# Out projection with the tokens as the moving side: 512-wide matmuls, rows restored by 16-bit DMA transposes

## Chip, cores and metric

One core of a Trainium2 chip. The metric is the device time of one launch in microseconds (us); less is better. The kernel before takes 814.0 us (median of 3 runs, 813.29 to 814.13). Engines: PE multiplies matrices, PEld is its weight load, DVE is VectorE, ACT is ScalarE, POOL is GpSimd, SP issues DMAs.

## The reference

Four batches, each with q, k, v of 6016 x 256. A 256 x 256 attention matrix per batch from column-normalised q and k, v times it, then a gated feed-forward block on all 24064 tokens:

```python
qn = q / (norm(q, axis=1) + 1e-6);  kn = k / (norm(k, axis=1) + 1e-6)
a  = softmax(kn^T @ qn / tau)              # 256 x 256 per batch
x  = v @ a                                 # 24064 x 256 over all batches
out = (silu(x @ w_gate) * (x @ w_val)) @ w_out    # hidden width 1536
```

## The kernel before

`a` is folded into the weights (`Wg`, `Wv`), so a chunk of 4x128 tokens (the last of a batch has 3x128) passes three products: gate, value, out. A chunk has 12 steps, one per 128 of the hidden width. In each step PE does two gate matmuls and two value matmuls for this chunk, then four out matmuls for the chunk before. ACT makes the silu, DVE the product `sv`. In the background q and k of the next batch are squared (DVE, ACT), summed (POOL) and multiplied.

```python
class OutStage:                                  # one per chunk; cut
    def emit(self, count):
        for _ in range(count):
            j, f = divmod(self.at, FH)           # j: 128 tokens, f: 128 of the hidden width
            if f == 0 and j % 2 == 0:
                self.o_ps = psum_o.tile([P, 2, C], FP32, tag="o")
            nc.tensor.matmul(self.o_ps[:, j % 2, :],
                             self.sv[:, f, j * P:(j + 1) * P],     # stationary: tokens
                             w_out_sb[:, f, :],                    # moving: 256 columns
                             start=(f == 0), stop=(f == FH - 1))
            # ... after two j: one fp32 copy (ACT for the first pair, DVE for the second), one store

for gi, (b, ci) in enumerate(allc):              # 48 chunks
    for f in range(FH):
        g_ps, v_ps, mv = gv_matmuls(b, ci, f)    # 4 matmuls, 512 wide
        silu = gv_silu(g_ps, mv)
        gv_product(f, sv, silu, v_ps, mv)
        if prev is not None: prev.emit(prev.cm)  # 4 out matmuls, 256 wide
        if b + 1 < B: background(b + 1, ci * FH + f)
        # ... load_v two chunks ahead
    prev = OutStage(b, ci, sv)
```

Of the kernel before, what the change touches and what calls it, by code (L numbers as in the profile page):

```python
# [8 lines left out]
FP32 = mybir.dt.float32  # L9
BF16 = mybir.dt.bfloat16  # L10
FP8 = mybir.dt.float8e5
ALU = mybir.AluOpType
ACT = mybir.ActivationFunctionType
DR = mybir.MatmulPerfMode.DoubleRow
# [3 lines left out]
def kernel(  # L18
# [11 lines left out]
    nc = tc.nc  # L30
    P = 128

    B, N, C = q.shape
    D, DFF = moe_w_gate.shape
    assert C == D and C == 2 * P
    CH = C // P
    FH = DFF // P
# [8 lines left out]
    CS = 4  # L46
# [3 lines left out]
    chunks = [(s, min(CS, NS - s)) for s in range(0, NS, CS)]  # L50
    NCH = len(chunks)
    STEPS = NCH * FH
    groups = [(s, min(4, NS - s)) for s in range(0, NS, 4)]
# [9 lines left out]
    svpool = ctx.enter_context(tc.tile_pool(name="svpool", bufs=2))  # L63
    silupool = ctx.enter_context(tc.tile_pool(name="silupool", bufs=4))
    opool = ctx.enter_context(tc.tile_pool(name="opool", bufs=4))
    dram = ctx.enter_context(tc.tile_pool(name="dram", bufs=4, space=bass.MemoryType.DRAM))

    psum_gv = ctx.enter_context(tc.tile_pool(name="psum_gv", bufs=2, space=bass.MemoryType.PSUM))
    psum_o = ctx.enter_context(tc.tile_pool(name="psum_o", bufs=2, space=bass.MemoryType.PSUM))
# [23 lines left out]
    w_out_sb = const.tile([P, FH, C], BF16)  # L93
# [5 lines left out]
    def load_qk(b, g, which, gl=groups):  # L99
        if b not in qk_tiles:  # L100
            q_sb = qkpool.tile([P, NS, C], FP8, tag="q_sb")
            k_sb = qkpool.tile([P, NS, C], FP8, tag="k_sb")
            qk_tiles[b] = (q_sb, k_sb)
# [3 lines left out]
            out=dst[:, gs:gs + gm, :],  # L107
            in_=src[b].rearrange("(p s) c -> p s c", s=NS)[:, gs:gs + gm, :])

    def load_v(b, ci):  # L110
        cs, cm = chunks[ci]
        mv = cm * P
        vb = dram.tile([CS * P, C], BF16, tag="vb")
        nc.gpsimd.dma_start(  # L114
            out=vb[:mv, :].rearrange("(p s) c -> p (s c)", s=cm),
            in_=v[b, cs * P:cs * P + mv, :].rearrange("(p s) c -> p (s c)", s=cm))
        vT = vpool.tile([P, CH, CS * P], BF16, tag="vT")
        nc.sync.dma_start_transpose(out=vT[:, :, :mv], in_=vb[:mv, :])
        vt_ready[(b, ci)] = vT
# [16 lines left out]
    def evacuate_first_v(h):  # L136
        nc.vector.tensor_copy(vt_ready[(0, 0)][:, h, :], state["vt_ps"][:, h, :])
# [82 lines left out]
    def first_softmax(b):  # L220
        kq, ink = state[b, "kq"], state[b, "ink"]
        inq = work.tile([P, CH], FP32, tag="inq")
        first_root(inq, state[b, "cols"])
        s_f = work.tile([P, CH, C], FP32, tag="s_f")
        nc.vector.tensor_mul(s_f[:, 0, :], kq[:, 0, :], ink)
        nc.vector.tensor_scalar_add(inq, in0=inq, scalar1=1e-6)
        nc.vector.reciprocal(inq, inq)
        if inv_tau != 1.0:
            nc.vector.tensor_scalar_mul(inq, in0=inq, scalar1=inv_tau)
        nc.vector.tensor_mul(s_f[:, 1, :], kq[:, 1, :], ink)  # L230
        rs = psum_m.tile([P, CH], FP32, tag="misc")
        keep_warm(1)
        row_eps(rs)
        transpose_first_v()
        keep_warm(2)
        for h in range(CH):
            evacuate_first_v(h)
        exT = attn.tile([P, CH, C], BF16, tag="exT")
        state[b, "exT"] = exT
        for jh in range(CH):  # L240
            nc.scalar.activation(exT[:, jh, :], s_f[:, jh, :], ACT.Exp,
                                 scale=inq[:, jh:jh + 1])


        def row_sum(jh):
            for ih in range(CH):
                nc.tensor.matmul(rs[:, ih:ih + 1], exT[:, jh, ih * P:(ih + 1) * P],
                                 ones_bf[:, 0:1], start=False,
                                 stop=(jh == CH - 1), skip_group_check=True)

        units = []
        for u in range(2 * CH):
            unit_ps = psum_gv.tile([P, HW], FP32, tag="gv"[u % 2])
            units.append(unit_ps)
        row_sum(0)
        wp_matmul(b, 0, 0, units[0], lo)
        wp_matmul(b, 1, 0, units[1], lo)
        wp_matmul(b, 2, 0, units[2], lo)
        row_sum(1)
        finish_rs(b, rs)  # L260
        for u, jh in ((0, 1), (1, 1), (2, 1), (3, 0), (3, 1)):
            wp_matmul(b, u, jh, units[u], lo)
        for u in range(4):
            wp_evacuate(b, u, units[u], lo, u % 2 == 1)
        for u in range(2):
            wp_unit(b, u, psum_o, "o", hi)
        nc.scalar.preload_act_table(ACT.Silu)

    def norm_acc(b, t):
# [5 lines left out]
        if t == 0:  # L275
            acc_new = work.tile([P, 2, C], FP32, tag="acc")
            state[b, "acc"] = acc_new
            nc.gpsimd.tensor_tensor(out=acc_new, in0=sq[:, 0, :, :], in1=sq[:, 1, :, :],  # L278
                                    op=ALU.add)
            return  # L280
        acc = state[b, "acc"]
        for s in range(pm):
            nc.gpsimd.tensor_tensor(out=acc, in0=acc, in1=sq[:, s, :, :], op=ALU.add)  # L283

    def split3(src, shape, tag):
# [6 lines left out]
        nc.gpsimd.tensor_copy(hi, src)  # L292
        nc.gpsimd.tensor_tensor(out=rest, in0=src, in1=hi, op=ALU.subtract)
        nc.gpsimd.tensor_copy(mid, rest)
        nc.gpsimd.tensor_tensor(out=lo, in0=rest, in1=mid, op=ALU.subtract)
        return hi, mid, lo
# [4 lines left out]
    def norm_cols(b):  # L301
# [8 lines left out]
        nc.vector.tensor_copy(inv, cs)  # L310
        nc.gpsimd.tensor_tensor(out=inv, in0=inv, in1=half, op=ALU.pow)  # L311
        nc.gpsimd.tensor_scalar_add(inv, in0=inv, scalar1=1e-6)
        nc.gpsimd.tensor_tensor(out=inv, in0=inv, in1=minus, op=ALU.pow)
        state[b, "inv"] = inv
# [97 lines left out]
    def gv_matmuls(b, ci, f):  # L412
        cs, cm = chunks[ci]
        mv = cm * P
        Wg, Wv = state[b, "W"]
        vT = vt_ready[(b, ci)]
        fs = slice(f * P, (f + 1) * P)
        g_ps = psum_gv.tile([P, CS * P], FP32, tag="g")
        v_ps = psum_gv.tile([P, CS * P], FP32, tag="v")
        for dst, W in ((g_ps, Wg), (v_ps, Wv)):  # L420
            for kk in range(CH):
                nc.tensor.matmul(dst[:, :mv], W[:, kk, fs], vT[:, kk, :mv],  # L422
                                 start=(kk == 0), stop=(kk == CH - 1))
        return g_ps, v_ps, mv
# [6 lines left out]
    def gv_product(f, sv, silu, v_ps, mv):  # L431
        nc.vector.tensor_mul(sv[:, f, :mv], silu[:, :mv], v_ps[:, :mv])  # L432

    class OutStage:


        def __init__(self, b, ci, sv):
            cs, self.cm = chunks[ci]
            self.sv = sv

            pat = "(p s) c -> p s c" if (b, ci) == (0, 0) else "(s p) c -> p s c"
            r0 = b * N + cs * P
            self.dst = out[r0:r0 + self.cm * P, :].rearrange(pat, p=P)
            self.at = 0
            self.n = self.cm * FH
            self.o_ps = None

        def emit(self, count):
            for _ in range(count):
# [41 lines left out]

    LOAD0, SQ0 = 9, 21
    plan = [[] for _ in range(STEPS)]
    for g in range(len(groups)):
        plan[LOAD0 + 5 * g].append((load_qk, g, 0))
        plan[LOAD0 + 5 * g].append((load_qk, g, 1))
    for t in range(NP):
        step = SQ0 + (5 * t) // 2
        plan[step].append((norm_acc, t))
# [14 lines left out]
        plan[S1 + 36 + (u * 3) // 2].append((wp_unit, u))  # L514

    def background(b, step):
        for what, *args in plan[step]:
            what(b, *args)

    def load_w(c0, c1):  # L520
        cols = slice(c0, c1)
# [5 lines left out]
    allc = [(b, ci) for b in range(B) for ci in range(NCH)]  # L527
    VT_AHEAD = 2
# [19 lines left out]
    load_w(0, HW)  # L548
    load_w(HW, WP)
    load_v(*allc[1])  # L550
    for wc in range(1, NWC):
        load_w(wc * WP, (wc + 1) * WP)
    nc.gpsimd.dma_start(out=w_out_sb, in_=moe_w_out.rearrange("(h l) d -> l h d", l=P))
# [2 lines left out]
    for g, which, gl in order:  # L556
# [23 lines left out]
        if which == 0:  # L580
# [6 lines left out]
            if G_COLS <= g < NQ - 2:  # L587
                keep_warm(NQ - 2 - g)
    first_softmax(0)
    prev = None  # L590
    for gi, (b, ci) in enumerate(allc):
        sv = svpool.tile([P, FH, CS * P], BF16, tag="sv")
        for f in range(FH):
            g_ps, v_ps, mv = gv_matmuls(b, ci, f)


            us = range(2 * f + 2, min(2 * f + 4, len(wp_units))) if gi == 0 else ()
            part = hi if f == 0 else full
            for u in us[:1]:
                wp_unit(0, u, psum_o, "o", part, on_dve=True)  # L600
            silu = gv_silu(g_ps, mv)
            for u in us[1:]:
                wp_unit(0, u, psum_o, "o", part, on_dve=(f == 0))
            gv_product(f, sv, silu, v_ps, mv)
            if prev is not None:
                prev.emit(prev.cm)
            if b + 1 < B:
                background(b + 1, ci * FH + f)
            if f == 0 and gi + VT_AHEAD < len(allc):
                load_v(*allc[gi + VT_AHEAD])  # L610
        prev = OutStage(b, ci, sv)
    prev.finish()


# [1 line left out]
_INS = ['q', 'k', 'v', 'tau', 'moe_w_gate', 'moe_w_val', 'moe_w_out']  # L616
# [31 lines left out]
```

## Time and profile before

| | kernel before |
|---|---|
| time, median (range) | 814.0 us (813.29 to 814.13) |
| PE busy, waits of PE after 48 us | 98%, none |
| DVE, ACT, POOL busy | 65%, 53%, 32% |
| 16 DMA engines busy | 47% of the span by packet times |

The lines that carry this are in the prediction.

### The profile page before, as it was taken

How to read it: one execution, taken by the hardware profiler on the slowest of the kernel's cores; microseconds unless marked ns; L12 is line 12 of the kernel's file. 1: busy time of each engine (PE TensorE's matmuls, PEld its weight loads, DVE VectorE, ACT ScalarE, POOL GpSimd, SP SyncE). 2: the span in 40 equal slices, each digit the busy share in tenths (PEclk: the TensorE clock that was granted, in tenths of full speed). 3: DMA queues.
4: the chain of work that ended last, by engine and by line, in shares of the span. 5: the costliest groups of instructions: out<-in, count | busy, mean ns of one | idle time of the engine just before them, and what ended most of it. 6: DMA issues, size and time to landing. Idle time of an engine off the chain costs nothing.

```text
span 811.5 us, 13757 instructions
## 1 busy us (share of the span) xinstructions
PE 796.4 (98%) x5047; PEld 489.0 (60%) x5047; DVE 524.1 (65%) x795; ACT 433.9 (53%) x757; POOL 262.7 (32%) x320
## 2 busy tenths in 40 slices
PE   4999999999999999999999999999999999999998
PEld 2656666665566666666565666666556566665666
DVE  4777777657556777756655677765765555555554
ACT  4665655545555656545545556654555544444543
POOL 4415887323000888723000488752300000000000
PEclk9999999999999999999999999999999999999999
DMA  9994875319211778325812378531952122122101
GB/s 89 144 154 76 107 105 88 78 34 154 74 40 46 97 101 106 74 65 97 126 40 59 53 87 120 90 79 32 182 96 66 46 51 54 53 40 65 50 27 59
DMA packets 92308, 64.99 MB, mean 80 GB/s; under 512 B 52737, under 2 KB 89857, under 8 KB 91489
## 3 DMA queue, kind: packets, MB, share of 16 engines
q0 software_dynamic: 18144, 27.41, 29.1%
q1 hardware_dynamic: 73952, 36.65, 17.8%
q8 instruction: 39, 0.64, 0.3%
q14 instruction: 29, 0.23, 0.1%
q10 hardware_dynamic: 144, 0.07, 0.0%
HBM read 79.04 MB, written 36.70 MB: 143 GB/s over the span
## 4 chain that ended last, share of the span: by engine, by line
PE 96%; DMA 3%; issue 0%; DVE 0%; POOL 0%; POOLq 0%
PE o_new L456 30%; PE g_ps L422 30%; PE v_ps L422 30%; PE ps L391 2%; DMA q_sb<-in_q_dram 2%; PE kq_new L151 2%; DMA k_sb<-in_k_dram 1%; PE ps L381 0%; PE last_ps L480 0%; PE ss_new L178 0%; PE kq_new L156 0%; PE unit_ps L391 0%; PE cs L307 0%; POOL k_sb L106 0%; PE cols L191 0%
## 5 line engine op out<-in xcount | busy, mean ns | idle before, releaser
L432 DVE TENSOR_TENSOR sv<-silu,v_ps 128x512 bf16<-128x512 bf16 (+1 forms) x576 | 388.3, 674 | 263.1 <-ACT silu L428 260.4
L428 ACT ACTIVATE silu<-g_ps 128x512 bf16<-128x512 f32 (+1 forms) x576 | 338.7, 588 | 323.4 <-PE g_ps L422 291.9
L456 PE MATMUL o_new<-w_out_sb,sv 128*128 128x256 bf16 x2244 | 337.2, 273 | 0.0
L422 PE MATMUL g_ps<-vT,Wg 128*128 128x512 bf16 (+1 forms) x1128 | 330.7, 375 | 0.0
L422 PE MATMUL v_ps<-vT,Wv 128*128 128x512 bf16 (+1 forms) x1128 | 330.4, 374 | 0.0
L456 PEld LDWEIGHTS <-sv 128*128 128x128 bf16 x2244 | 219.6, 98 | 140.6
L422 PEld LDWEIGHTS <-Wv 128*128 128x128 bf16 x1152 | 112.7, 98 | 130.7 <-ACT Wv L403 0.2
L283 POOL TENSOR_TENSOR acc_new<-acc_new,sq 128x512 f32<-128x512 f32 x135 | 158.3, 1173 | 42.7 <-DVE sq L273 34.3
L422 PEld LDWEIGHTS <-Wg 128*128 128x128 bf16 x1152 | 109.6, 98 | 25.0
L273 DVE TENSOR_TENSOR sq<-q_sb 128x512 bf16<-128x512 fp8e5 x72 | 67.0, 930 | 0.0
L278 POOL TENSOR_TENSOR acc_new<-sq 128x512 f32<-128x512 bf16 x3 | 3.5, 1155 | 152.0 <-DVE sq L273 152.0
L274 ACT ACTIVATE sq<-k_sb 128x512 bf16<-128x512 fp8e5 x72 | 44.2, 614 | 0.0
L465 ACT COPY o_sb<-o_new 128x512 f32<-128x512 f32 x48 | 28.1, 586 | 14.9 <-PE o_new L456 14.5
L151 PE MATMUL kq_new<-k_sb,q_sb 128*128 128x512 fp8e5 x184 | 31.6, 298 | 1.0 <-DMA q_sb<-in_q_dram 0.9
L467 DVE COPY o_sb<-o_new 128x512 f32<-128x512 f32 (+1 forms) x47 | 31.3, 666 | 0.0
L106 POOL DMA_DIRECT2D q_sb<-in_q_dram x45 | 25.3, 562 | 14.8 <-DMA k_sb<-in_k_dram 9.9
L106 POOL DMA_DIRECT2D k_sb<-in_k_dram x42 | 22.8, 544 | 10.4 <-DMA w_out_sb<-in_moe_w_out_dram 5.5
L114 POOL DMA_DIRECT2D vb<-in_v_dram x47 | 24.0, 514 | 5.3 <-DMA vb<-in_v_dram 3.5
L178 PE MATMUL ss_new<-sq,ones_bf 128*128 128x256 bf16 x83 | 14.6, 332 | 11.1 <-ACT sq L168 11.1
L151 PEld LDWEIGHTS <-q_sb 128*128 128x256 fp8e5 x184 | 21.8, 140 | 2.8 <-DMA q_sb<-in_q_dram 2.0
L178 PEld LDWEIGHTS <-ones_bf 128*128 128x128 bf16 x83 | 9.2, 116 | 15.0 <-issue 11.0
L311 POOL TENSOR_TENSOR inv<-inv,half 128x4 f32<-128x4 f32 x3 | 3.1, 1036 | 36.7 <-DVE inv L310 36.7
(94 smaller groups left out, 198.3 us busy)
## 6 DMA issues: line engine op xcount, KB each, us to landing
out_dram<-o_sb SPq DMA_DIRECT2D x92, 256.0 KB, 2.5
vb<-in_v_dram POOLq DMA_DIRECT2D x43, 256.0 KB, 5.5
q_sb<-in_q_dram POOLq DMA_DIRECT2D x36, 128.0 KB, 4.5
k_sb<-in_k_dram POOLq DMA_DIRECT2D x33, 128.0 KB, 5.7
k_sb<-in_k_dram POOLq DMA_DIRECT2D x5, 256.0 KB, 9.0
q_sb<-in_q_dram POOLq DMA_DIRECT2D x4, 256.0 KB, 18.4
w_out_sb<-in_moe_w_out_dram POOLq DMA_DIRECT2D x1, 768.0 KB, 13.6
vb<-in_v_dram POOLq DMA_DIRECT2D x4, 192.0 KB, 3.9
```

Source lines behind the costliest of these rows:

```text
L106: nc.gpsimd.dma_start(out=dst[:, gs:gs + gm, :], in_=src[b].rearrange("(p s) c -> p s c", s=NS)[:, gs:gs + gm, :])
L114: nc.gpsimd.dma_start(out=vb[:mv, :].rearrange("(p s) c -> p (s c)", s=cm), in_=v[b, cs * P:cs * P + mv, :].rearrange("(p s) c -> p (s c)" ...
L151: nc.tensor.matmul(kq[:, jh, :], q_sb[:, ps:ps + 2, js], k_sb[:, ps:ps + 2, :], start=(t == 0 and jh == 0), stop=last, perf_mode=DR, skip_ ...
L273: nc.vector.tensor_mul(sq[:, :pm, 0, :], q_sb[:, ps:ps + pm, :], q_sb[:, ps:ps + pm, :])
L274: nc.scalar.activation(sq[:, :pm, 1, :], k_sb[:, ps:ps + pm, :], ACT.Square)
L283: nc.gpsimd.tensor_tensor(out=acc, in0=acc, in1=sq[:, s, :, :], op=ALU.add)
L422: nc.tensor.matmul(dst[:, :mv], W[:, kk, fs], vT[:, kk, :mv], start=(kk == 0), stop=(kk == CH - 1))
L428: nc.scalar.activation(silu[:, :mv], g_ps[:, :mv], ACT.Silu)
L432: nc.vector.tensor_mul(sv[:, f, :mv], silu[:, :mv], v_ps[:, :mv])
L456: nc.tensor.matmul(self.o_ps[:, j % 2, :], self.sv[:, f, j * P:(j + 1) * P], w_out_sb[:, f, :], start=(f == 0), stop=(f == FH - 1))
L465: nc.scalar.copy(o_sb[:, :m, :], self.o_ps[:, :m, :])
L467: nc.vector.tensor_copy(o_sb[:, :m, :], self.o_ps[:, :m, :])
```

## The change

Its intent is to halve the number of out matmuls: `w_out` becomes the stationary side and the tokens move, 512 at a time. The result then stands in columns (256 channels by tokens), and must be turned to rows. The DMA transpose takes 16-bit data, so each fp32 half is copied as two 16-bit planes, stored to DRAM, transposed back and stored as fp32. The last two chunks keep the old stage. To make room for these transfers, q and k of later batches are loaded over a longer time, and v passes through two fixed DRAM buffers and is transposed six steps after its load.

```diff
+class OutColumns:                               # cut
+    def step(self):                             # two matmuls per step
+        h, f = divmod(self.at, FH)
+        nc.tensor.matmul(self.o_ps[h][:, :self.mv], w_out_sb[:, f, h * P:(h + 1) * P],
+                         self.sv[:, f, :self.mv], start=(f == 0), stop=(f == FH - 1))
+    def copy(self, h):                          # at steps 5 and 11 of the chunk
+        halves = self.o_ps[h].bitcast(U16).rearrange("p (n t) -> p t n", t=2)
+        nc.scalar.copy(pl[:, 0, :self.mv], halves[:, 0, :self.mv])
+        nc.vector.tensor_copy(pl[:, 1, :self.mv], halves[:, 1, :self.mv])
+    def spill(self, h):                         # 2 steps later, SP
+        nc.sync.dma_start(out=rows[...], in_=self.planes[h][...])
+    def transpose(self, h):                     # 3 steps later, SP
+        nc.sync.dma_start_transpose(out=self.ot[...], in_=self.planes[h][...])
+    def store(self):
+        nc.sync.dma_start(out=self.dst, in_=self.ot[:, :self.cm, :].bitcast(FP32))
 ...
-        vb = dram.tile([CS * P, C], BF16, tag="vb")
+        vb = vb_tiles[(b * NCH + ci) % 2]
 ...
+            if b + 1 < B:                       # q and k of batch b + 1, half of them earlier
+                for what, *args in early_loads[step]: what(b + 1, *args)
 ...
-        prev = OutStage(b, ci, sv)
+        prev = (OutColumns if gi < len(allc) - 2 else OutStage)(b, ci, sv)   # shortened
```

More of the change, by code (lines that the diff above doesn't have):

```diff
@@ L11 @@
 FP8 = mybir.dt.float8e5
+U16 = mybir.dt.uint16
 ALU = mybir.AluOpType
@@ L65 @@
     opool = ctx.enter_context(tc.tile_pool(name="opool", bufs=4))
+    ocpool = ctx.enter_context(tc.tile_pool(name="ocpool", bufs=2))
+    plpool = ctx.enter_context(tc.tile_pool(name="plpool", bufs=4))
     dram = ctx.enter_context(tc.tile_pool(name="dram", bufs=4, space=bass.MemoryType.DRAM))
+    dram_v = ctx.enter_context(tc.tile_pool(name="dram_v", bufs=1, space=bass.MemoryType.DRAM))
     psum_gv = ctx.enter_context(tc.tile_pool(name="psum_gv", bufs=2, space=bass.MemoryType.PSUM))
@@ L108, in load_qk @@
             in_=src[b].rearrange("(p s) c -> p s c", s=NS)[:, gs:gs + gm, :])
+    vb_loaded = {}
+    vb_tiles = []
+    for n in range(2):
+        vb_new = dram_v.tile([CS * P, C], BF16, tag="vb%d" % n)
+        vb_tiles.append(vb_new)
     def load_v(b, ci):
@@ L116, in load_v, with transpose_v @@
             in_=v[b, cs * P:cs * P + mv, :].rearrange("(p s) c -> p (s c)", s=cm))
+        vb_loaded[(b, ci)] = vb
+    def transpose_v(b, ci):
+        mv = chunks[ci][1] * P
+        vb = vb_loaded.pop((b, ci))
         vT = vpool.tile([P, CH, CS * P], BF16, tag="vT")
@@ L432, in gv_product, with out_rows, __init__ @@
         nc.vector.tensor_mul(sv[:, f, :mv], silu[:, :mv], v_ps[:, :mv])
+    def out_rows(b, ci):
+        cs, cm = chunks[ci]
+        pat = "(p s) c -> p s c" if (b, ci) == (0, 0) else "(s p) c -> p s c"
+        r0 = b * N + cs * P
+        return out[r0:r0 + cm * P, :].rearrange(pat, p=P)
+    class OutColumns:
+        def __init__(self, b, ci, sv):
+            self.cm = chunks[ci][1]
+            self.mv = self.cm * P
+            self.sv = sv
+            self.dst = out_rows(b, ci)
+            self.at = 0
+            self.o_ps = [None] * CH
+            self.planes = [None] * CH
+            self.ot = None
+        def step(self):
+            for _ in range(CH):
+                h, f = divmod(self.at, FH)
+                if f == 0:
+                    o_new = psum_o.tile([P, CS * P], FP32, tag="o")
+                    self.o_ps[h] = o_new
+                nc.tensor.matmul(self.o_ps[h][:, :self.mv],
+                                 w_out_sb[:, f, h * P:(h + 1) * P],
+                                 self.sv[:, f, :self.mv],
+                                 start=(f == 0), stop=(f == FH - 1))
+                self.at += 1
+        def copy(self, h):
+            halves = self.o_ps[h].bitcast(U16).rearrange("p (n t) -> p t n", t=2)
+            pl = plpool.tile([P, 2, CS * P], U16, tag="pl")
+            nc.scalar.copy(pl[:, 0, :self.mv], halves[:, 0, :self.mv])
+            nc.vector.tensor_copy(pl[:, 1, :self.mv], halves[:, 1, :self.mv])
+            self.planes[h] = pl
+        def spill(self, h):
+            rows = dram.tile([2 * P, CS * P], U16, tag="rows%d" % h)
+            nc.sync.dma_start(
+                out=rows[:, :self.mv].rearrange("(p t) n -> p t n", t=2),
+                in_=self.planes[h][:, :, :self.mv])
+            self.planes[h] = rows
+        def transpose(self, h):
+            if self.ot is None:
+                ot_new = ocpool.tile([P, CS, 2 * C], U16, tag="ot")
+                self.ot = ot_new
+            nc.sync.dma_start_transpose(
+                out=self.ot[:, :self.cm, h * 2 * P:(h + 1) * 2 * P],
+                in_=self.planes[h][:, :self.mv])
+        def store(self):
+            nc.sync.dma_start(out=self.dst, in_=self.ot[:, :self.cm, :].bitcast(FP32))
@@ L434 @@
     class OutStage:
         def __init__(self, b, ci, sv):
-            cs, self.cm = chunks[ci]
+            self.cm = chunks[ci][1]
             self.sv = sv
-            pat = "(p s) c -> p s c" if (b, ci) == (0, 0) else "(s p) c -> p s c"
-            r0 = b * N + cs * P
-            self.dst = out[r0:r0 + self.cm * P, :].rearrange(pat, p=P)
+            self.dst = out_rows(b, ci)
             self.at = 0
@@ L446, in __init__, with step @@
             self.o_ps = None
+        def step(self):
+            self.emit(self.cm)
         def emit(self, count):
@@ L493 @@
     plan = [[] for _ in range(STEPS)]
+    first_loads = [[] for _ in range(STEPS)]
+    early_loads = [[] for _ in range(STEPS)]
+    late_loads = [[] for _ in range(STEPS)]
+    half_g = len(groups) // 2
     for g in range(len(groups)):
-        plan[LOAD0 + 5 * g].append((load_qk, g, 0))
-        plan[LOAD0 + 5 * g].append((load_qk, g, 1))
+        for which in range(2):
+            first_loads[LOAD0 + 5 * g].append((load_qk, g, which))
+            step = 7 + 11 * (g - half_g)
+            if step < 0:
+                early_loads[step + STEPS].append((load_qk, g, which))
+            else:
+                late_loads[step].append((load_qk, g, which))
     for t in range(NP):
@@ L516, in background @@
     def background(b, step):
-        for what, *args in plan[step]:
+        loads = first_loads if b == 1 else late_loads
+        for what, *args in loads[step] + plan[step]:
             what(b, *args)
+        if b + 1 < B:
+            for what, *args in early_loads[step]:
+                what(b + 1, *args)
     def load_w(c0, c1):
@@ L550 @@
     load_v(*allc[1])
+    transpose_v(*allc[1])
     for wc in range(1, NWC):
@@ L589, with at_step @@
     first_softmax(0)
+    later = {}
+    def at_step(n, what, *args):
+        later.setdefault(n, []).append((what, args))
     prev = None
@@ L593 @@
         for f in range(FH):
+            now = gi * FH + f
             g_ps, v_ps, mv = gv_matmuls(b, ci, f)
@@ L605 @@
             if prev is not None:
-                prev.emit(prev.cm)
+                prev.step()
             if b + 1 < B:
@@ L610 @@
                 load_v(*allc[gi + VT_AHEAD])
-        prev = OutStage(b, ci, sv)
+                at_step(now + 6, transpose_v, *allc[gi + VT_AHEAD])
+            for what, args in later.pop(now, ()):
+                what(*args)
+        if gi < len(allc) - 2:
+            prev = OutColumns(b, ci, sv)
+            n0 = (gi + 1) * FH
+            for h in range(CH):
+                n = n0 + FH // CH * (h + 1) - 1
+                at_step(n, prev.copy, h)
+                at_step(n + 2, prev.spill, h)
+                at_step(n + 5, prev.transpose, h)
+            at_step(n0 + 22, prev.store)
+        else:
+            prev = OutStage(b, ci, sv)
     prev.finish()
```

## The prediction

> **What bounds the kernel now.** I read the busy shares and the chain that ended last first, then PE's waits, then the groups, then the timeline.
>
> ```profile
> PE 796.4 (98%) x5047; PEld 489.0 (60%) x5047; DVE 524.1 (65%) x795; ACT 433.9 (53%) x757; POOL 262.7 (32%) x320
> ...
> PE 96%; DMA 3%; issue 0%; DVE 0%; POOL 0%; POOLq 0%
> ```
>
> The chain is PE for 96% of the span; the DMA part is the loading before about 28 us. All waits of PE in the execution:
>
> ```profile
> PE ss_new L178 <- ACT sq L168: 11.1, 6, 7.3
> PE kq_new L151 <- DMA q_sb<-in_q_dram: 0.9, 2, 0.5
> ```
>
> Both lines are of the prologue (columns: us in total, times, longest). From 48 us on PE waits for nothing, so only PE's own stream can be shortened. The matmuls of the timeline, start and length first:
>
> ```profile
> 190.22 0.60 PE L456 MATMUL o_new<-w_out_sb,sv 128*128 128x256 bf16 x4
> 190.65 0.59 PE L422 MATMUL g_ps<-vT,Wg 128*128 128x512 bf16 x2
> 191.09 0.59 PE L422 MATMUL v_ps<-vT,Wv 128*128 128x512 bf16 x2
> 191.52 0.60 PE L456 MATMUL o_new<-w_out_sb,sv 128*128 128x256 bf16 x4
> ```
>
> One step (one of 12 slices of the hidden width) is 1.30 us in thirds of 0.43: gate, value, out. The lengths overlap, so I use distances between starts: over all starts in the trace 109.2 ns after a 256-wide out matmul (1652 pairs of neighbours), 216.0 ns after a 512-wide one, 162.5 ns after a 384-wide one. Cross-check: the chain gives o_new 30.2% of 811.5 us, over 2244 matmuls 109.2 ns.
>
> ```profile
> L456 PE MATMUL o_new<-w_out_sb,sv 128*128 128x256 bf16 x2244 | 337.2, 273 | 0.0
> L456 PEld LDWEIGHTS <-sv 128*128 128x128 bf16 x2244 | 219.6, 98 | 140.6
> L465 ACT COPY o_sb<-o_new 128x512 f32<-128x512 f32 x48 | 28.1, 586 | 14.9 <-PE o_new L456 14.5
> L467 DVE COPY o_sb<-o_new 128x512 f32<-128x512 f32 (+1 forms) x47 | 31.3, 666 | 0.0
> ```
>
> A weight load takes 98 ns, less than the 109 ns of the matmul that it runs beside; it is hidden. The 337.2 us in the first row are not PE time to be won.
>
> **What the Trainium skill says.** "TensorE: Matmul & The Clock Gate", section "Wait — 56ns, not 53.3ns?": warm matmuls follow each other at N ÷ 2.4 GHz plus about 2.5 ns, fixed per matmul. That is 109.2 ns for 256 and 215.8 for 512: the trace agrees (109.2 and 216.0). "DMA: Bandwidth & Descriptors", section "Constraints" (DMA transpose): 2-byte types only, destination in SBUF; so an fp32 result goes as two 16-bit planes and through DRAM. The trace shows such transposes for v alone. Same page, "Issuing engines are not separate DMA queues": all transfers share 16 engines; the trace agrees in so far as both queues' packets lie on the same 16. "PSUM — Partial Sum Buffer", "Terms": ScalarE and VectorE may not read one bank at once. No run shows it yet, but in the built program each new VectorE copy waits for the ScalarE copy of the other plane.
>
> **The change part by part.**
>
> PE. There are 48 chunks, 44 of 4x128 tokens and 4 of 3x128. The last two keep the old stage. The other 46 (43 full, 3 short) give up 43x48 + 3x36 = 2172 narrow matmuls for 46x24 = 1104 wide ones. The columns streamed are the same. A full chunk costs 48x109.2 = 5241 ns before, 24x216.0 = 5184 after: 57 ns less; times 43, 2.5 us. A short one 36x109.2 = 3931 against 24x162.5 = 3900: 0.03 us, times 3, 0.1 us. The sum is 2.6 us, 0.31%. Check by the fixed part: 1068 fewer matmuls times about 2.5 ns are 2.7 us (an estimate with the TensorE page's figure). About 1068 weight loads also go (105 us of PEld at 98 ns), worth nothing, being hidden.
>
> ACT and DVE. Each chunk had one copy on each; now two on each, 16-bit from PSUM with a stride of two. I take the old rows, as the element count is 512 as before: 46x0.586 = 27 us more ACT, 46x0.68 = 31 us more DVE. Their shares become 57% and 68%: no new bound on average, so the question is local. The value product has a margin: normally it starts every 1.30 us, takes 0.69 us, and its PSUM buffer is written again two steps on. The value matmuls started at 188.49; the product on them would at normal pace run from 189.37 to 190.06, and the buffer's next writer starts at 188.49 + 2.60 = 191.09. The margin is 1.03 us. The worst place of before is the four reciprocals, once per batch for three batches:
>
> ```profile
> 192.34 0.63 DVE L432 TENSOR_TENSOR sv<-silu,v_ps 128x512 bf16<-128x512 bf16 x1
> 192.89 0.94 DVE L344 RECIPROCAL den<-den 128x128 f32<-128x128 f32 x1
> 193.74 0.63 DVE L432 TENSOR_TENSOR sv<-silu,v_ps 128x512 bf16<-128x512 bf16 x1
> ```
>
> Four steps from the product at 188.07 normal pace would be 193.27; it is 193.74, 0.47 late, and PE doesn't wait. The built program now has a DVE copy (0.60 from start to start) after the third reciprocal: 1.07 late, so a wait of 0.05 to 0.2 us, times 3. The same may happen where a copy meets a slow square (up to 1.33 us long in the trace): four meetings per batch, two of them new, with 0.61 + 1.25 + 0.60 - 1.30 = 1.16 us late, a wait of 0.1 to 0.2 each. I allow 0.3 us for all.
>
> PSUM for out. Two tiles in turn, each filled in 6 steps (7.8 us), copied in under 2 us: never short.
>
> DMA. Added: 43x512 KB + 3x384 KB = 23.7 MB spilled to DRAM and as much transposed.
>
> ```profile
> q0 software_dynamic: 18144, 27.41, 29.1%
> q1 hardware_dynamic: 73952, 36.65, 17.8%
> ...
> vT<-vb SPq DMA_TRANSPOSE x47, 3.9
> ```
>
> By the trace's packets, a transpose of before moves 256 B in 23.4 ns and a store 1 KB in 49.1 ns. So 92,700 more transpose packets are 136 us of 16 engines (16.7% of the span), and 23,200 spill packets 71 us (8.8%): the sum goes from 47% to 73%. Per stretch of time (busy us and instructions of PE, PEld, DVE, ACT, POOL, then the granted clock) the DMA share is the last number but one:
>
> ```profile
> 70.00:140.00 70.00, 70.00 (x444) 43.19 (x442) 53.38 (x75) 42.44 (x75) 58.32 (x63) 1.00 0.69 98
> 620.00:800.00 180.00, 180.00 (x1118) 109.15 (x1116) 102.40 (x154) 89.09 (x153) 0.00 (x0) 1.00 0.19 49
> ```
>
> The first, where batch 1's q and k are loaded in their old places, goes to 0.95. It stays under the 1.12 that the prologue keeps up over 48 us. Slack is long: q and k are asked for 12 steps (15.6 us) before use and land in 5.4 us at the median; v is transposed 18 steps (23 us) before use; a plane buffer is reused after four halves (31 us), while spilling takes some 4 us (estimate from stores' 2.5 and transposes' 3.9). Even twice the landing time reaches no engine.
>
> Loads of q and k for later batches, and v's two fixed buffers. These spread traffic that hides already: nothing gained on PE, only insurance for the added transfers. Prologue (48 us) and last two chunks are unchanged.
>
> Sum: 814.0 - 2.6 + 0.3 = 811.7 us.
>
> **Rivals.**
>
> 1. Weight loads do cost something, and halving them pays: up to 1068x98 ns = 105 us, a time near 709. For it: PEld is busy 60%. Against: the starts are at streaming distance to the nanosecond, and 256-wide and 512-wide fit one line with 2.5 ns. Very unlikely.
>
> 2. ACT and DVE become a wait: the VectorE copy waits for the ScalarE copy, and both keep back the next silu and product. A copy that takes 1.2 us instead of 0.68 (16-bit strided reads were never timed here) would exceed the margin at perhaps ten places per loaded batch by 0.5 us: 15 us, time 826. For it: DVE is at 90% beside the reciprocals. Against: at most steps DVE is idle 0.61 us, and the margin is 1.03.
>
> 3. DMA becomes the wait: at 0.95 the loads of batch 1 land more than 15.6 us after issue, the squares wait, DVE is in order, PE waits. If each of 12 groups cost 1 us: 823. For it: the change itself spreads loads and delays the transposes of v, as if that had been needed. Against: the slacks above; and in 620 to 800 us, a fifth of the run, DMA would be under half busy.
>
> 4. Nothing: the 2.6 us are eaten by waits of the size of rival 2: 814.
>
> **Range and chances.** PE's stream is packed, so time cannot fall much below 811.4; runs of before spread 0.8 us, which makes the low end 810.7. The high end, 814.8, allows 3 us of waits. Rivals 2 and 3 together get 5% of being worse than 830; rival 1 gets 1%. Faster by over 2%: 0.01; within 2%: 0.94; slower: 0.05.
>
> **What would show it.** The starts of the new out matmuls stand 216 ns apart; PE's list of waits still has only the prologue's lines, or DVE products and silu with some tenths of a us; the chain stays near 96% PE; copies at 0.59 and 0.68 us; DMA share near 0.73. It is wrong if PE waits for sv, silu, vT or o tiles by more than 3 us, if a copy takes over 1 us, or if DVE's squares wait for q in batches 1 to 3.

## More of the kernel before

To compare traces I cut the run at two starts of matmuls: the first gate matmul of the second chunk and that of the very last step. The part between, 563 steps of the main loop, I call the **steady stretch**. In the kernel before it begins at 52.33 us, lasts 750.94 us, and 9.99 us follow it.

## The result, and the profile after

811.9 us (median of 4 runs, 811.27 to 813.92) against 814.01 in the same rounds: ratio 0.998, interval 0.9961 to 1.0. Ratios here are the mean time of one kernel's fast runs over that of the other's fast runs of the same rounds, so not quite the ratio of the medians quoted; a run counts as slow when it is over 1.5% above the fastest of its kernel. 0.2% is at the edge of what such runs resolve, so the traces must say whether it is the predicted 0.2%.

The busy shares and the chain that ended last, from the page after:

```profile
PE 790.1 (98%) x3905; PEld 385.5 (48%) x3979; DVE 550.1 (68%) x841; ACT 455.6 (56%) x803; POOL 260.9 (32%) x320
...
PE 95%; DMA 3%; issue 1%; ACT 0%; DVE 0%; POOL 0%; ACTq 0%; POOLq 0%
```

PEld fell from 60% to 48% and PE stayed at 98%: the freed weight loads were not PE time. (PE counts 3905 matmuls beside 3979 weight loads: 74 matmul records are missing from this trace.) All of PE's waits after:

```profile
PE ss_new L195 <- ACT sq L185: 11.1, 6, 7.3
PE kq_new L168 <- DMA q_sb<-in_q_dram: 0.9, 2, 0.5
PE cols L218 <- issue: 0.2, 1, 0.2
```

They are the prologue's, as before. The groups of the new out stage (busy us, mean ns of one, idle before):

```profile
L480 PE MATMUL o_new<-sv,w_out_sb 128*128 128x512 bf16 (+1 forms) x1078 | 318.9, 375 | 1.2
...
L490 DVE COPY pl<-o_new 128x512 uint16<-128x512 uint16 (+1 forms) x92 | 62.3, 677 | 9.5 <-ACT pl L489 9.5
...
L489 ACT COPY pl<-o_new 128x512 uint16<-128x512 uint16 (+1 forms) x92 | 53.2, 578 | 19.3 <-PE o_new L480 17.2
```

A 16-bit copy with a stride of two out of PSUM costs what the fp32 copy of as many elements cost (677 and 578 ns against 666 and 586). DVE's copy waits for ACT's copy of the other plane, 9.5 us in all.

Around the reciprocals of batch 1, DVE:

```profile
191.06 0.94 DVE L361 RECIPROCAL den<-den 128x128 f32<-128x128 f32 x1
191.91 0.63 DVE L490 COPY pl<-o_new 128x512 uint16<-128x512 uint16 x1
192.46 0.67 DVE L449 TENSOR_TENSOR sv<-silu,v_ps 128x512 bf16<-128x512 bf16 x1
193.05 0.95 DVE L361 RECIPROCAL den<-den 128x128 f32<-128x128 f32 x1
193.91 0.63 DVE L449 TENSOR_TENSOR sv<-silu,v_ps 128x512 bf16<-128x512 bf16 x1
```

The product at 187.65 is on pace; four steps of 1.295 us later would be 192.83, and it starts at 193.91, 1.08 us late. It ends at 194.54. PE at that place:

```profile
194.09 0.59 PE L439 MATMUL g_ps<-vT,Wg 128*128 128x512 bf16 x2
194.59 0.59 PE L439 MATMUL v_ps<-vT,Wv 128*128 128x512 bf16 x2
```

The value matmuls start 0.50 us after the gate matmuls instead of 0.43, 0.05 us after the product's end. By the starts in the trace the gap is 66, 67 and 68 ns at the three batches. The list of waits, which shows nothing here, is too coarse for it.

The transfers after:

```profile
q1 hardware_dynamic: 182720, 84.11, 44.0%
q0 software_dynamic: 18144, 27.41, 31.6%
...
ot_new<-rows SPq DMA_TRANSPOSE x92, 3.7
```

Together 0.76 of the 16 engines. By stretch (70 to 140 us; 620 to 800 us; the DMA share is the last number but one):

```profile
70.00:140.00 70.00, 69.63 (x338) 33.80 (x344) 56.24 (x79) 44.42 (x79) 58.30 (x64) 1.00 0.99 161
...
620.00:800.00 180.00, 179.16 (x856) 85.07 (x871) 109.58 (x165) 94.79 (x166) 3.90 (x8) 1.00 0.56 129
```

How much slack is left shows on SP, whose issues follow one another in program order. It stood 274.8 us in all before transposes of out, until their spills had landed:

```profile
SPq L504 <- DMA rows<-pl: 274.8, 92, 10.3
```

The transposes of v stand in the same queue. By their landings in the trace, v was ready at the least 3.0 us before PE needed it (median 18.5); in the kernel before, at the least 12.5 us (median 23.1).

**Where the time went.** The profiled runs took 813.27 us before and 811.27 after:

| part | before | after | difference |
|---|---|---|---|
| to the second chunk's first gate matmul | 52.33 | 52.40 | +0.07 |
| steady stretch | 750.94 | 748.47 | -2.48 |
| after it | 9.99 | 10.40 | +0.41 |
| sum | 813.26 | 811.27 | -2.00 |

The steady stretch is hardly noisy: the changed kernel, profiled again in the experiments, gave 748.468 us both times, to the nanosecond. The step fell from 1300 to 1295 ns at the median.

The last row was not foreseen. Both kernels end with a store from SP; here are the last SP issues before, after, and of the last experiment below, whose spans are 811.5, 809.5 and 808.8 us:

```profile
809.01 0.34 SPq L489 DMA_DIRECT2D out_dram<-last_sb  x1
```

```profile
806.60 0.34 SPq L566 DMA_DIRECT2D out_dram<-last_sb  x1
```

```profile
806.27 0.34 SPq L567 DMA_DIRECT2D out_dram<-last_sb  x1
```

From that store to the end it takes 2.5, 2.9 and 2.5 us. In the trace's records SP then checks nine semaphores in the same order in all three, 60 to 70 ns apart when nothing is to be waited for. In the kernel before, the last store raises the last of them; in the changed kernel it raises the third, and six checks follow its landing: 0.36 us.

### The profile page after: what moved, and what is told of

It reads as the page before. It is cut to its first block, busy times and chain, and to the rows that moved or that the text cites. A ratio compares the mean times of both kernels' runs of the same rounds, so it can differ in the third digit from the quotient of the medians.

```text
span 809.5 us, 11903 instructions
## 1 busy us (share of the span) xinstructions
PE 790.1 (98%) x3905; PEld 385.5 (48%) x3979; DVE 550.1 (68%) x841; ACT 455.6 (56%) x803; POOL 260.9 (32%) x320
## 4 chain that ended last, share of the span: by engine, by line
PE 95%; DMA 3%; issue 1%; ACT 0%; DVE 0%; POOL 0%; ACTq 0%; POOLq 0%
PE g_ps L439 30%; PE v_ps L439 30%; PE o_new L480 29%; PE ps L408 2%; DMA q_sb<-in_q_dram 2%; PE kq_new L168 2%; PE o_new L533 1%; DMA k_sb<-in_k_dram 1%; ACT silu L445 0%; PE last_ps L557 0%; DVE sv L449 0%; PE ss_new L195 0%; PE kq_new L173 0%; PE ps L398 0%; PE unit_ps L408 0%
## 5 line engine op out<-in xcount | busy, mean ns | idle before, releaser
L439 PE MATMUL v_ps<-vT,Wv 128*128 128x512 bf16 (+1 forms) x1109 | 326.3, 374 | 1.2
L439 PE MATMUL g_ps<-vT,Wg 128*128 128x512 bf16 (+1 forms) x1105 | 325.8, 375 | 1.3
L480 PE MATMUL o_new<-sv,w_out_sb 128*128 128x512 bf16 (+1 forms) x1078 | 318.9, 375 | 1.2
L300 POOL TENSOR_TENSOR acc_new<-acc_new,sq 128x512 f32<-128x512 f32 x135 | 156.1, 1156 | 56.0 <-DVE sq L290 41.9
L480 PEld LDWEIGHTS <-w_out_sb 128*128 128x128 bf16 x1104 | 108.0, 98 | 126.3
L126 POOL DMA_DIRECT2D vb_new<-in_v_dram x47 | 24.2, 516 | 265.5 <-DMA vT<-vb_new 264.6
L490 DVE COPY pl<-o_new 128x512 uint16<-128x512 uint16 (+1 forms) x92 | 62.3, 677 | 9.5 <-ACT pl L489 9.5
L489 ACT COPY pl<-o_new 128x512 uint16<-128x512 uint16 (+1 forms) x92 | 53.2, 578 | 19.3 <-PE o_new L480 17.2
L168 PE MATMUL kq_new<-k_sb,q_sb 128*128 128x512 fp8e5 x184 | 35.6, 319 | 0.9 <-DMA q_sb<-in_q_dram 0.9
L408 PEld LDWEIGHTS <-exT 128*128 128x128 bf16 x104 | 10.0, 98 | 10.9 <-DMA w_gate_sb<-in_moe_w_gate_dram 0.2
```

Of the source, the lines that this page charges most:

```text
L168: nc.tensor.matmul(kq[:, jh, :], q_sb[:, ps:ps + 2, js], k_sb[:, ps:ps + 2, :], start=(t == 0 and jh == 0), stop=last, perf_mode=DR, skip_ ...
L300: nc.gpsimd.tensor_tensor(out=acc, in0=acc, in1=sq[:, s, :, :], op=ALU.add)
L408: nc.tensor.matmul(ps, state[b, "exT"][:, jh, ih * P:(ih + 1) * P], (w_gate_sb, w_val_sb)[w][:, jh, cols], start=(jh == 0), stop=(jh == CH ...
L439: nc.tensor.matmul(dst[:, :mv], W[:, kk, fs], vT[:, kk, :mv], start=(kk == 0), stop=(kk == CH - 1))
L480: nc.tensor.matmul(self.o_ps[h][:, :self.mv], w_out_sb[:, f, h * P:(h + 1) * P], self.sv[:, f, :self.mv], start=(f == 0), stop=(f == FH - 1))
L489: nc.scalar.copy(pl[:, 0, :self.mv], halves[:, 0, :self.mv])
```

## The experiments

Twelve runs in three groups. Each group shares its runs of the kernel before (medians 814.32, 813.49 and 814.09 us; these runs fall into two clusters, near 813.3 and 814.3, which moves the median).

**The changed kernel again (control).**

> The changed kernel once more, unedited, as the control of this group: 811 to 812.5 us, 0.2 to 0.3% under the kernel before. It also shows how much its runs scatter: 811.27 to 813.92 so far, against 0.8 us for the kernel before.

Measured: 811.36 us (811.27 to 812.38), ratio 0.9975 (0.9962 to 0.9989); steady stretch 748.468 us. The gain is there, and is 0.25%.

**Wide matmuls alone.** The result is in the wrong order, on purpose.

```diff
-        prev = OutStage(b, ci, sv)
+        prev = (OutWide if gi < len(allc) - 2 else OutStage)(b, ci, sv)
+    # OutWide: two 512-wide matmuls per step as in OutColumns, then as before one fp32 copy per
+    # half (ACT, DVE) and one store of the columns; no planes, no spill, no transpose
```

> The kernel before with wide out matmuls alone: one fp32 copy per half as before, columns stored as they are (result in the wrong order on purpose), no second copy, no spill, no transpose of out. Theory (the length of PE's stream decides; copies and transfers are hidden but for 0.2 us at the reciprocals): 814.0 - 2.8 = 811.2 us, within 0.5 us of the changed kernel, PE gaps at the reciprocals gone. Rival (the added copies and transfers cost something, and the real worth of the wide matmuls is larger and was partly eaten): clearly below the changed kernel, 810 us or less.

Measured: 811.67 us (810.78 to 811.74), ratio 0.9971 (0.9959 to 0.9984). Steady stretch 748.273 us, 2.67 less than before, without gaps at the reciprocals; 10.00 us after it. So 2.67 us is all that the wide matmuls can give, and the added copies and 47 MB of transfers take 0.195 of it away in the steady stretch. The rival (a larger gain, partly eaten) is out. That the median is no lower than the changed kernel's lies in the prologue: the profiled run reached the second chunk at 53.43 us.

**Cut in two, all else kept.**

```diff
+                for n0 in range(0, self.mv, 256):
+                    n1 = min(n0 + 256, self.mv)
-                nc.tensor.matmul(self.o_ps[h][:, :self.mv], ...
+                    nc.tensor.matmul(self.o_ps[h][:, n0:n1], ...   # moving side sv[:, f, n0:n1]
```

> The changed kernel with each wide out matmul cut in two of 256 tokens, all else kept: matmuls and weight loads of out are back at the old number, copies, spills and transposes stay. Theory (a fixed 2.5 ns per matmul): the gain is gone, 811.9 + 1104 x 2.6 ns = 814.8 us, or 814.2 to 815. Rival (the gain came from the loads and the layout and not from the number of matmuls): stays at 811.9.

Measured: 813.99 us (813.86 to 815.6), ratio 1.0006 (0.9993 to 1.0018); steady stretch 751.13 us, of which 3 x 36 ns are gaps at the reciprocals. The gain is gone with the number of matmuls alone: 751.13 - 0.11 - 748.27 = 2.75 us for 1104 more, 2.5 ns each. Layout, loads and buffers have no part in it.

**Cut in four.** The same edit with 128.

> The changed kernel with each wide out matmul cut in four of 128 tokens: 4344 instead of 1104 out matmuls and weight loads in these chunks. Theory (a fixed 2.5 ns per matmul, and weight loads of 98 ns overlap each other as well as the matmuls, as in the last out tile of the kernel before, where 128-wide matmuls start 56 ns apart): (4 x 55.8 - 215.8) ns x 1032 + 0.5 us for the short chunks = 8.1 us more, 820 us. Rival 1 of the prediction (a weight load of 98 ns must fit behind a matmul): 98 ns each, (4 x 98 - 216) ns x 1032 = 182 us more, about 995 us.

Measured: 819.29 us (819.08 to 819.37), ratio 1.0067 (1.0054 to 1.008). Its out matmuls, eight in a step, with a weight load each:

```profile
193.54 0.59 PE L439 MATMUL v_ps<-vT,Wv 128*128 128x512 bf16 x2
193.98 0.61 PE L482 MATMUL o_new<-sv,w_out_sb 128*128 128x128 bf16 x8
194.42 0.59 PE L439 MATMUL g_ps<-vT,Wg 128*128 128x512 bf16 x2
```

Eight take 0.44 us, 56 ns each, though a weight load is recorded with 98 ns. So loads overlap each other, and rival 1 is out even where the matmul is shorter than the load. The steady stretch is 756.46 us, 8.2 more than with the wide matmuls alone (3240 more matmuls, 2.5 ns each).

**The insurance taken away.** q and k of all later batches in the old places, v through the old pool, its transpose issued at once.

```diff
-        loads = first_loads if b == 1 else late_loads
-        for what, *args in loads[step] + plan[step]:
+        for what, *args in first_loads[step] + plan[step]:
 ...
-        vb = vb_tiles[(b * NCH + ci) % 2]
+        vb = dram.tile([CS * P, C], BF16, tag="vb")
 ...
-                at_step(now + 6, transpose_v, *allc[gi + VT_AHEAD])
+                transpose_v(*allc[gi + VT_AHEAD])
```

> The changed kernel with q and k of all later batches loaded in the old places, v through the old pool of DRAM buffers, and v's transposes issued at once: the insurance taken away. Theory (15 to 23 us of slack, all hidden): the same as the changed kernel within 0.5 us, PE waits only in the prologue. Rival (the loads had to be spread once out's traffic was added): DVE's squares wait for q, PE waits for products, 815 to 825 us.

Measured: 812.41 us (811.65 to 814.43), ratio 0.9986 (0.9973 to 0.9998); steady stretch 748.652 us. One new wait of 0.19 us for a product (at 484 us); that is all the insurance buys in this trace. It has a price as well: with the transposes issued at once, v was ready at the least 7.0 us before its use; in the changed kernel, where they come six steps later, 3.0 us (0.3 to 4.0 in five other traces with its plan of transfers).

**DVE's copy twice.** A test of the margin of 1.03 us.

```diff
+            nc.vector.tensor_copy(px[:, :self.mv], halves[:, 1, :self.mv])   # nothing reads px
```

> The changed kernel with VectorE's 16-bit copy of each half done twice (0.60 us more from start to start, twice per chunk). Theory (a product may be about 1.03 us late before PE waits): at the reciprocals the lateness goes from 1.07 to 1.67, a wait of 0.65 us, 3 times, 2 us; where a copy meets a square of 1.2 to 1.3 us, up to 0.6 us in at most 12 places; nothing at all in batch 3. In all 2 to 6 us slower. Rival (the margin does not decide, PE waits only where DVE is full on average): under 1 us slower.

Measured: 817.02 us (815.93 to 817.37), ratio 1.0037 (1.0024 to 1.005); steady stretch 754.01 us, 5.5 longer. PE's list of waits now has a line that it had not, and the wait stands in PE's timeline:

```profile
PE v_ps L439 <- DVE sv L449: 2.8, 7, 0.6
```

```profile
194.74 0.59 PE L439 MATMUL v_ps<-vT,Wv 128*128 128x512 bf16 x2 [0.39 <-DVE sv L449]
```

By the starts of matmuls, the reciprocals cost 0.55 + 0.12 us in each of three batches (0.65 was expected), and 3.8 us fall on 15 other places, most of them where copies meet squares. PE waits here while DVE is 73% busy: the margin decides, not the average.

**Reciprocals moved off the copy.**

```diff
-        plan[S1 + 29 + n].append((recip, n))
+        plan[S1 + (28, 29, 30, 32)[n]].append((recip, n))
```

> The changed kernel with the four reciprocals of a batch at other steps (one step earlier, and none in the step of the copy). Theory: the three gaps of 67 ns on PE go away, 0.2 us faster, which is under the scatter of the times, so it is to be read from the starts of the matmuls in the trace; time 811.7. Rival (the gaps have another cause): the gaps stay or move.

Measured: 812.86 us (811.23 to 815.66), ratio 0.9991 (0.9977 to 1.0005). The step that follows the last reciprocal is on pace, value 0.43 us after gate:

```profile
193.99 0.59 PE L439 MATMUL g_ps<-vT,Wg 128*128 128x512 bf16 x2
194.42 0.59 PE L439 MATMUL v_ps<-vT,Wv 128*128 128x512 bf16 x2
```

Steady stretch 748.273 us, exactly that of the wide matmuls alone: the three gaps were the whole price of the added copies and transfers there. The median is above the control's, because the profiled run reached the second chunk at 54.88 us instead of 52.40. In all profiled runs that kept their schedule the steady stretch and the end add up to the account above, and only this start differs (52.3 to 54.9 us; here PE also waited 2.7 us for q instead of 0.9). So the scatter of the times sits in the prologue, as far as profiled runs show; why some executions start late isn't settled.

**Spills and transposes of out twice.** How much DMA reserve is left?

```diff
+                at_step(n + 2, prev.again, h)         # the same planes to another DRAM tile
                 at_step(n + 5, prev.transpose, h)
+                at_step(n + 5, prev.again_back, h)    # transposed into a tile that nothing reads
```

> The changed kernel with every spill of out and every transpose of out done twice, the second into a tile that nothing reads: some 25% of the span more on the 16 DMA engines, from 0.76 to 1.0 on average and to about 1.25 in the stretch where batch 1 is loaded. Theory (long slack): at most 1 us slower. Rival 3 (transfers are near the limit): the sync queue, which waits for each spill before it transposes, or the loads fall behind, and PE waits: 5 us or more slower.

Measured: 870.45 us, ratio 1.0606 (1.0573 to 1.0638); its runs scatter from 859.91 to 874.84, two are fast (mean 863.1) and the profiled one is slow. My theory failed by 50 us. PE's longest wait in total, from the profiled, slow run:

```profile
PE g_ps L440 <- DMA vT<-vb_new: 43.3, 13, 13.5
```

PE waits for transposed v. After the longest waits PE also runs at half speed for some 4 us (starts 0.42 to 0.43 us apart instead of 0.22), as the Trainium skill has it ("TensorE: Matmul & The Clock Gate", "What's actually happening": an idle window halves the clock); the granted clock was 0.97. Three runs ask what ran out.

**Four plain spills per half, no further wait.**

```diff
+            for i in range(3):                        # SP, nothing waits for them
+                nc.sync.dma_start(out=rows_x[...], in_=self.pl_kept[h][...])
```

> Why did spilling and transposing twice cost 7%? The changed kernel with each half spilled four times: three more plain stores of 256 KB per half, which nothing waits for: about 26% of the span more on the 16 DMA engines, as much as in the doubled run, but no further wait and little issue time on the sync queue. Theory A (the one sync queue, in order, with its waits for spills and 1.25 us per transpose, falls behind and v comes late): under 2 us slower than the changed kernel. Theory B (the 16 engines are full): 10 us or more slower.

**Transposes twice from the same rows.**

```diff
+                at_step(n + 5, prev.again_back, h)
```

> The changed kernel with each transpose of out done twice from the same rows, no further spill: some 17% of the span more on the DMA engines and 2.5 us more issue time per chunk on the sync queue, no further wait for a spill. Theory A: between nothing and 10 us slower, the waits of PE, if any, for v and after the 10 us in which nothing lands beside the small store of the k norms. Theory B: about two thirds of the doubled run's 57 us.

**Both twice, without the small store of the k norms.** Only nearly the right result, on purpose.

```diff
-        nc.gpsimd.dma_start(out=row.rearrange("(h p) -> p h", p=P), in_=inv[:, CH:])
-        nc.gpsimd.dma_start(out=ink, in_=row.partition_broadcast(P))
+        nc.gpsimd.memset(ink, 0.1289)
```

> The doubled run (spills and transposes of out twice) without the store of the row of k norms to DRAM in 4-byte pieces and its load back; a constant near the norms takes their place, so the result is only nearly right, on purpose. In all traces no packet moves for some 10 us behind that store, and in the doubled run PE's two longest waits, of 12.6 and 13.7 us, follow it. Theory (that standstill is what breaks the sync queue's schedule): those long waits go, the time falls from 870 to 840 us or less. Rival (the standstill only marks the place where the queue is late anyway): 860 us or more.

Measured: spills four times 843.94 us, ratio 1.0359 (1.0343 to 1.0375); transposes twice 843.26 us, ratio 1.0383 (1.0338 to 1.0428); without the small store 854.52 us, fast runs 848.91 and 841.56, ratio 1.0384 (1.0348 to 1.042), profiled run slow. PE's wait for v in the three:

```profile
PE g_ps L439 <- DMA vT<-vb_new: 20.6, 9, 7.5
```

```profile
PE g_ps L440 <- DMA vT<-vb_new: 17.3, 7, 5.4
```

```profile
PE g_ps L439 <- DMA vT<-vb_new: 40.4, 17, 8.3
```

Theory A, as I had put it, is out: it needed further waits on the sync queue, and plain spills that nothing waits for cost 31 us. Theory B, full engines, fits better, and the stretches show where. First the changed kernel, then the run with four spills, twice:

```profile
140.00:300.00 160.00, 159.15 (x772) 75.88 (x787) 110.95 (x170) 90.89 (x162) 54.03 (x67) 1.00 0.83 144
```

```profile
140.00:300.00 160.00, 152.31 (x735) 70.84 (x733) 102.70 (x159) 84.70 (x151) 46.41 (x60) 0.98 1.06 218
...
620.00:800.00 180.00, 180.00 (x854) 83.38 (x852) 110.51 (x168) 95.93 (x167) 5.37 (x11) 1.00 0.96 244
```

With q and k of the next batch being loaded, the share went from 0.83 to 1.06 and PE lost 8 us of 160; in the last batch, where nothing of that is loaded, PE stayed busy at a share of 0.96. (PE's 159.15 in the changed kernel is due to the missing records.) But it is not one threshold: the transposes twice had a share of only 0.95 in the same stretch and cost as much, in spite of a third less added engine time, and part of the doubled run's loss is of another kind. Behind the small store of norms (256 values of 4 bytes), hardly a packet moves for some 7 us, whichever queue it belongs to (in the traces of before, after, wide alone and doubled, at batch 1; the 10 us of the expectations was too much). Other transfers also land late: at batch 3 of the kernel before, the 256 packets of a store were through at 558.97 us and it landed at 566.27. 1 KB packets that began then in the doubled run took up to 7.5 us instead of 0.05. Without that store packets flow at this place, and the fast runs of the doubled kernel (two of each) fall from 863.1 to 845.2 us: a third of its excess, less than I expected and more than the rival did. That the standstill itself costs this isn't shown: the edit also takes away the load back and POOL's wait of 11.5 us for the store, during which POOL issues no other load. So the reserve is below 17% of the span on the engines.

The order of the one sync queue is in it as well; the traces of the two runs with fast profiles (four spills, transposes twice) show how. At all 15 of PE's waits for v over 0.5 us there, v's plain load had landed 11 to 27 us before its transpose was issued, and SP issued the transpose within 0.1 us of coming to it: SP was late. The longest wait of the four-spill run:

```profile
389.49 6.85 SPq L497 DMA_DIRECT2D rows<-pl  x1
396.39 3.81 SPq L506 DMA_DIRECT2D rows<-pl  x3
411.14 1.23 SPq L514 DMA_TRANSPOSE ot_new<-rows  x1
412.47 1.24 SPq L135 DMA_TRANSPOSE vT<-vb_new  x1
```

v had been loaded at 396.8 us. The issue of the first spill alone took 6.85 us. SP then issued the others and stood from 400.3 to 411.1, until the first of these spills had landed, then transposed out, and only then v; PE waited until 415.75. So, as these traces show it, spills land late on the busy engines, and the queue's order hands the delay on to v. That is theory A's path, driven by theory B's load. No run reorders the queue, so how much would be left without it stays open.

**Best version: reciprocals moved, and the last store's semaphore shifted.**

```diff
+            if gi == 40 and f < 6:       # six 64-byte loads that only shift the semaphores
+                nc.sync.dma_start(out=pad_sb[:, f * 16:(f + 1) * 16], in_=q[0, 0:1, 0:16])
```

> The changed kernel with the reciprocals moved, as in e8, and with six 64-byte loads on the sync queue late in the run that only shift which semaphore the last store gets. Theory: the three waits of 65 ns go and the last store is again checked last, as in the kernel before, so that six checks of 60 ns no longer follow it: from the first gate product of the last step to the end 10.0 us instead of 10.4. Lowest time 811.27 - 0.2 - 0.4 = 810.7 us, median by the luck of the prologue up to 812. Rival (the end is longer for another reason): the end stays at 10.4 us.

Measured: 811.69 us (810.55 to 814.76), ratio 0.9977 (0.9963 to 0.9991), no gap in the steady stretch (748.274 us) and 10.01 us after it. Both accounts hold, and 810.55 us is the lowest time of all correct kernels; its median is not below the control's, most likely because the prologue's scatter is larger than the 0.58 us gained. It beats both kernels in its parts, not provably in its median.

## Why the prediction was right

811.7 us was predicted, 811.9 measured. Point by point:

- **PE's stream decides.** Shown: with the matmul count back, the gain is gone (cut in two); with wide matmuls and nothing else, it is whole.
- **The term of 2.6 us.** Measured 2.67. The 216.0 ns that I took for a 512-wide matmul held a few longer distances; 2.5 ns per matmul is confirmed at 128, 256 and 512 columns.
- **Weight loads are worth nothing.** Right, but for a wrong reason. I argued that 98 ns is less than the 109 ns of a matmul. Cut in four, 98 ns loads stand behind matmuls 56 ns apart and cost nothing either. The trace before had it too: its last out tile, 128 wide, has starts 56 ns apart.
- **The margin of 1.03 us and the wait at the reciprocals.** 0.05 to 0.2 us each was predicted for a lateness of 1.07; it was 1.08 late and 65 to 68 ns of wait. The copy done twice confirmed the margin.
- **Copies meeting slow squares.** A wait of 0.1 to 0.2 us at some of these places was allowed for, and none came: without the three gaps at the reciprocals the steady stretch equals that of the wide matmuls alone.
- **Sizes of copies and transfers.** DVE 677 ns and ACT 578 ns against 680 and 586; DMA share 0.76 against 0.73, and 0.99 against 0.95 in the stretch of batch 1.
- **"Even twice the landing time reaches no engine."** After the prologue no transfer made PE wait, but the argument was wrong. The 23 us for v were counted from the planned step and left out what SP waits for before it gets there: the least slack was 3.0 us. In that place the transpose landed 9.9 us after its issue, so twice that would have reached PE by about 7 us (estimate from these two). It was no measure of reserve either: a quarter of the span more of plain stores costs 31 us.
- **"All transfers share 16 engines."** The trace records a packet's queue and not its engine, so no run shows this part of what the prediction takes from the skill.
- **"Prologue and last two chunks are unchanged."** The end grew by 0.4 us through the order of the closing checks, about as much as I had set aside for waits that mostly did not come (0.3 allowed, 0.2 real). That the sum fits to 0.2 us is partly luck.

## What to carry to other kernels

When PE has no gap, wider matmuls win only the fixed cost per matmul: count the instructions that go, times the difference of start distances, and don't count busy time or weight loads. Before adding work to an engine with idle time, look for the one place where it already runs late, and compare the lateness with the margin that the double buffer leaves; it is also the cheapest place to mend. A transfer may be hidden at 0.76 of the DMA engines and still be close to the point where the queue falls behind, so double it once to see, and look at what stands before the urgent transfer in its queue.

## What the Trainium skill lacked or had wrong

- "TensorE: Matmul & The Clock Gate", section "Back-to-back issue gap": it gives about 81 ns per matmul for N=128 and about 131 for N=512 in a stream of weight loads and matmuls, and calls N ÷ 2.4 + 2.5 the isolated gap. Here streams with a weight load each ran at 56 ns (128), 109.2 (256) and 215.8 (512): the formula holds in the stream too.
- No page that I read gives this cost: a store of 256 values of 4 bytes to DRAM is followed by some 7 us in which hardly a packet of any queue moves, and transfers whose packets are through land up to 7.3 us later. Without it, and the load back, the doubled run is 18 us faster.
- "DMA: Bandwidth & Descriptors": no rule for how much load leaves latency-bound transfers alone. Here 0.83 over a batch's load phase cost PE nothing; 0.95 with transposes and 1.06 with plain stores cost about 30 us in the run, through the order of the one sync queue too.
- No page that I read has it: at the end of these kernels SP checks nine semaphores in a fixed order, 60 ns each, and a last store that raised the third instead of the last made the end 0.4 us longer.
- "PSUM — Partial Sum Buffer", "Terms" (no two engines on one bank at once): in the trace, DVE's copy of a bank waits for ACT's copy of the same bank, 9.5 us over 92 copies; the page gives no cost.
